# Attention with all score tiles turned by DMA, maxima taken in pairs, head pairs joined by a ratio of sums, and some MLP preparation on VectorE

## The chip, the core and the metric

The kernel runs on one core of a Trainium2 chip. The core has five engines, each working through its own list of instructions in order: TensorE (PE, with its weight loads shown apart as PEld), VectorE (DVE), ScalarE (ACT), GpSimd (POOL) and SyncE (SP), which here issues the DMAs. Engines wait for each other by semaphores. PE writes to PSUM, of which there are eight banks of 512 fp32 columns for each of 128 partitions; the other data lie in SBUF, and 16 DMA engines move data between DRAM and SBUF and within SBUF. The metric is the device time in microseconds.

## What is computed

An adaptive-layernorm block over 2048 rows of width 576, of attention and a gated MLP, in fp32. Cut to what matters here:

```python
h = _layernorm(x) * (1 + ca) + sa
q = h @ wq                                  # 32 heads of 128
k, v = the last 512 rows of 16 cached heads, each used by two query heads
p = softmax(q k^T / sqrt(128))              # 512 columns a row
x = x + ga * (concat(p v) @ wo)
h = _layernorm(x) * (1 + cb) + sb
x = x + gb * ((silu(h @ w1) * (h @ w3)) @ w2)   # inner width 4608
```

## The kernel before

**Precision.** PE multiplies fp16. A value in fp32 is split into a high fp16 half and a low one (the value less the high half), and each product is made of three matmuls: high by high, high by low and low by high.

**Slots.** The rows lie in four blocks of 512, the block in four tiles of 128 rows. The attention is a list `slots` of 128 entries, (use of a key head, query head `j` of its two, block). One slot is one query head on one block; slots 2p and 2p + 1 are the two heads of a pair on the same block, so the second head (`j` = 1) is always in an odd slot. The loop near the end of the kernel goes over slots `i` and steps `t` of 0 to 3 and writes the instructions of every engine in that order. No scheduler moves them: the order is that of the code.

**One slot's work.** `query` projects a slot ahead (14 matmuls in three parts, `QP`). `scores(i, t)` makes one tile of scores in a PSUM bank (tag S, two of them), and DVE takes the maximum of each row and a bias from it. `weights` makes the exponents on ACT, with their sums in `l`. The exponents have to be turned for the product with the values. For tiles 0 to 2, `half_high` (ACT) and `half_low` (POOL) split them to fp16 and `turn_away` (SP) turns them by a DMA transpose into `ptw`. Tile 3 goes another way: `turn` has PE turn it in fp32 by four transposes into a bank of tag T, a slot later, and `turn_high` (ACT) and `turn_low` (DVE) split it. `values(i - 1)` stands at the end of slot i, with 12 matmuls, and needs all four tiles.

**Sums.** `sums` takes the reciprocals, writes them to DRAM and reads them back to all partitions (`r`, 256 KB). `normalize`, two slots later, multiplies the product by them into `on`, `split_on` splits `on` in two halves `o` (ACT copy, POOL subtraction), and `attend_out` multiplies both heads of a pair by `wo` in one PSUM pair of banks `E`, from which DVE adds to `acc`.

**Preparation beside it.** Tasks put at steps (`at`, `run`) run after the step's own work: loads and splits of the next heads' weights, and the preparation of the MLP's weights. `make_set` makes sums and differences of blocks of w1 and w3 (Strassen-like products), `make_rows` multiplies rows of w2 by a gate and does the same. An item of that plan is a cast on ACT (`wmade`, `omade`) and subtractions on POOL. The table `WORK` spreads the items: full rate in slots 16 to 80, half in 80 to 104, 0.6 of it in 104 to 123. In the attention POOL does the sums and gates; for the last `FEW` = 8 blocks, which are made in the MLP, DVE does.

**Buffers.** `p` (PB) and `hp` (HF) have four buffers each, `ptw` two. A buffer is written again once its last reader has finished.

Of the kernel before, what the change touches and what calls it, by code (L numbers as in the profile page):

```python
# [9 lines left out]
F32 = mybir.dt.float32  # L10
# [12 lines left out]
DC = 4  # L23
# [20 lines left out]
Q_DOWN = 2.0**-17  # L44
EXPONENT = 0x7F800000
# [3 lines left out]
def tile_block(  # L49
# [27 lines left out]
    def bank(tag, name):  # L77
        return psum.tile([P, 512], F32, tag=tag, name=name)
# [4 lines left out]
    tpool = turning.enter_context(tc.tile_pool(name="tpool", bufs=2, space=PSUM))  # L83

    def t_bank():
        return tpool.tile([P, 512], F32, tag="T", name="pt")
# [149 lines left out]
    def turn_rows(b, m, tag):  # L236

        ps = t_bank() if tag == "T" else bank(tag, "ps_n")
# [202 lines left out]
    QP = (range(0, 5), range(5, 10), range(10, 14))  # L441
# [33 lines left out]
    def scores(i, t):  # L475
# [4 lines left out]
        rows = slice(t * P, (t + 1) * P)  # L480
        pss = bank("S", "pss")
        for n, (x, y) in enumerate(((0, 0), (0, 1), (1, 0))):
            nc.tensor.matmul(pss, q[:, x, rows], k[:, y, :], start=n == 0, stop=n == 2)  # L483
        m = (i * ST + t) % 3
        nm = nms[:, 2 * m : 2 * m + 2]
        factor = factors[:, g, j : j + 1]
        nc.vector.tensor_reduce(nm[:, 0:1], pss, axis=AX.X, op=ALU.max, negate=True)  # L487
        nc.vector.tensor_scalar(nm[:, 1:2], nm[:, 0:1], factor, P_LOG, op0=ALU.mult, op1=ALU.add)  # L488
        st["max", t] = pss, nm

    def weights(i, t):
# [5 lines left out]
        if t == 0:  # L497
            st["l"] = odd.tile([P, 2 * ST], F32, tag="l", name="l", bufs=3)
        p = pool.tile([P, SB], F32, tag="p", name="p", bufs=PB)
        nc.scalar.activation(p, pss, AF.Exp, bias=nm[:, 1:2], scale=factor, accum_out=st["l"][:, t : t + 1])  # L500
        st["p", t] = p

    def sums(i, step):

        st = state[i]
        if step == 0:
            nc.vector.reciprocal(st["l"][:, ST:], st["l"][:, :ST])
        elif step == 1:
            st["row"] = dram.tile([P, ST], F32, name=f"row{i}")
            nc.sync.dma_start(st["row"], st["l"][:, ST:])  # L510
# [5 lines left out]

    def turn(i, t):

        st = state[i]
        p = st.pop(("p", t))  # L520
        ps = st["t"] = t_bank().rearrange("p (j n) -> p j n", j=KC)
        for j in range(KC):
            nc.tensor.transpose(ps[:, j, :], p[:, j * P : (j + 1) * P], ident)  # L523

    def turn_high(i, t):
        st = state[i]
        nc.scalar.copy(st["pt"][:, 0, :, t * P : (t + 1) * P], st["t"])
# [6 lines left out]
    def half_low(i, t):  # L534

        hp = state[i]["hp", t]
        nc.gpsimd.tensor_sub(hp[:, 1, :], state[i].pop(("p", t)), hp[:, 0, :])  # L537
# [10 lines left out]

    def turn_low(i, t):
        cols = slice(t * P, (t + 1) * P)  # L550
        pt = state[i]["pt"]
        nc.vector.tensor_sub(pt[:, 1, :, cols], state[i]["t"], pt[:, 0, :, cols])  # L552
# [13 lines left out]

    def normalize(i):
# [9 lines left out]
    def split_on(i):  # L577
        st = state[i]
        on = st.pop("on")
        o = st["o"] = pool.tile([P, 2, SB], F16, tag=("ah", "al")[i % 2], name="o", bufs=3)  # L580
# [3 lines left out]
    def attend_out(pair, t, j, total):  # L584
        u, _, b = slots[2 * pair]
        back(state[2 * pair + j]["o"], wos[u][:, j], t, j == 0, j == 1)
        if j == 1:
# [3 lines left out]
                a, E[:, :, :HALF], factors[:, uses[u][0], 2:3], a, op0=ALU.mult, op1=ALU.add  # L591
# [164 lines left out]
    def make_set(f, n):  # L756
# [3 lines left out]
        if n < 0:  # L760
            eng = nc.vector if f >= NF - FEW else nc.gpsimd
            eng.tensor_add(s1, a21, a22)
            eng.tensor_sub(s2, s1, a11)
# [41 lines left out]
    def make_rows(p, n):  # L805
# [3 lines left out]
        if n < 0:  # L809
            if n < -2:  # L810
                r = whole[:, 2 * n + 8 : 2 * n + 10, :]
                eng = nc.vector if 2 * p >= NF - FEW else nc.gpsimd
                eng.tensor_mul(r, r, half_split(gates["b"]))
# [865 lines left out]
```

## Time and profile before

| | us |
|---|---|
| three runs, median | 2773.86 |
| lowest and highest | 2771.83 and 2776.18 |
| the profiled execution | 2773.59 |
| its span, first to last instruction | 2771.7 |
| first and last start of the values' matmuls (L562) | 61.7 and 1612.9 |

The profile is of one execution. A row of a group gives the line, the engine, the operation, output and input by name with partitions and elements, the count, busy time and the mean duration in ns, then the idle time just before and what ended it. A row of the timeline gives start, length, engine, line and names. In a row with three durations these are the least, the median and the largest. A row of the waits gives who waited for whom, then the total, the number of times and the longest. Matmuls are pipelined, with their ends modelled: the length of a matmul goes on past the start of the next.

### The profile page before, as it was taken

Reading aid. Unit: us, or ns where it says so; the run is one execution under the profiler, and the core shown is the slowest. Engines: PE = TensorE matmul, PEld = TensorE weight load, DVE = VectorE, ACT = ScalarE, POOL = GpSimd, SP = SyncE. Lnnn points to the kernel's source line nnn. Section 1 sums busy time; section 2 is a strip of 40 time slices with the busy share of each in tenths; the row PEclk is TensorE's granted clock in tenths of the full one; section 3 lists DMA queues with packets and bytes.
Section 4 is the critical chain, followed back from the end, with each engine's and each line's share of the span. In section 5 each row is a group of like instructions: output and inputs, shape, how many; then the busy total and the mean of one; then the engine's idle time right before and its main releaser. Section 6 shows DMA issues by size and latency. Waiting matters only on the chain.

```text
span 2771.7 us, 44752 instructions
## 1 busy us (share of the span) xinstructions
PE 2692.8 (97%) x15406; PEld 1515.9 (55%) x15406; DVE 1999.8 (72%) x3555; ACT 1617.5 (58%) x3013; POOL 1881.9 (68%) x1748
## 2 busy tenths in 40 slices
PE   6899999999999999999999999999999999999998
PEld 3455555555555555555555555555555555555554
DVE  7877787877788787877876667777776666666666
ACT  5777778777777778787677634544443333333332
POOL 5578788888788877777669537688873465333435
PEclk8999999999999999999999999999999999999999
DMA  5778888788787788979889935656643434333332
GB/s 184 174 174 195 196 177 192 169 184 192 160 185 167 191 186 201 206 182 213 184 190 223 239 112 171 200 170 199 213 135 108 160 121 128 104 103 111 104 110 78
DMA packets 593460, 463.84 MB, mean 167 GB/s; under 512 B 442704, under 2 KB 472528, under 8 KB 592208
## 3 DMA queue, kind: packets, MB, share of 16 engines
q1 hardware_dynamic: 592944, 460.69, 64.9%
q8 instruction: 121, 1.98, 0.3%
q14 instruction: 107, 0.88, 0.1%
q10 hardware_dynamic: 288, 0.30, 0.0%
HBM read 264.19 MB, written 95.99 MB: 130 GB/s over the span
## 4 chain that ended last, share of the span: by engine, by line
PE 52%; DVE 2%; issue 1%; ACT 1%; POOL 1%; DMA 0%; SPq 0%; DVEq 0%; ACTq 0%; POOLq 0%
PE py L847 15%; PE px L847 11%; PE pe L932 7%; PE pf L932 7%; PE pe L433 3%; PE po L562 3%; PE pss L483 3%; PE pq L410 2%; PE pt L523 0%; PE pq L414 0%; DVE table L487 0%; DVE acc L590 0%; DVE on L571 0%; DMA r<-row 0%; ACT p L500 0%
## 5 line engine op out<-in xcount | busy, mean ns | idle before, releaser
L537 POOL TENSOR_TENSOR hp<-p,hp 128x512 f16<-128x512 f32 x384 | 450.2, 1175 | 271.0 <-ACT hp L532 147.9
L500 ACT ACTIVATE p<-pss,table,factors 128x512 f32<-128x512 f32 x512 | 396.9, 775 | 360.9 <-DVE table L488 186.6
L847 PEld LDWEIGHTS <-wset 128*128 128x128 f16 x3528 | 344.6, 98 | 337.9 <-issue 5.3
L487 DVE TENSOR_REDUCE table<-pss 128x1 f32<-128x512 f32 x512 | 350.3, 684 | 209.9 <-PE pss L483 205.9
L847 PE MATMUL py<-hset,wset 128*128 128x512 f16 x2016 | 483.6, 380 | 0.0
L433 PE MATMUL pe<-o 128*128 128x288 f16 x3072 | 459.6, 286 | 15.8 <-DVE acc L590 15.3
L483 PE MATMUL pss<-k,qT 128*128 128x512 f16 x1536 | 420.1, 381 | 13.7 <-ACT p L500 10.3
L433 PEld LDWEIGHTS <-o 128*128 128x128 f16 x3072 | 300.7, 98 | 189.6 <-issue 22.4
L562 PE MATMUL po<-ptw,v 128*128 128x512 f16 x1536 | 359.3, 382 | 10.4 <-DVE ptw L552 5.5
L847 PE MATMUL px<-hset,wset 128*128 128x512 f16 x1512 | 361.6, 379 | 1.6 <-ACT p L500 1.6
L410 PE MATMUL pq<-hT,wq 128*128 128x512 f16 x1092 | 283.2, 382 | 1.0 <-POOL hT L254 0.7
L94 POOL TENSOR_TENSOR akv<-u,akv 128x512 f16<-128x512 f32 x141 | 165.0, 1180 | 174.3 <-ACT akv L93 166.5
L532 ACT CAST hp<-p 128x512 f16<-128x512 f32 x384 | 237.3, 618 | 13.2 <-POOL hT L256 0.6
L562 PEld LDWEIGHTS <-v 128*128 128x128 f16 x1536 | 148.2, 98 | 175.4 <-issue 19.4
L932 PEld LDWEIGHTS <-akv 128*128 128x128 f16 x1728 | 169.6, 98 | 93.8 <-issue 4.8
L483 PEld LDWEIGHTS <-qT 128*128 128x128 f16 x1536 | 147.9, 98 | 129.0 <-issue 15.6
L590 DVE SCALAR_TENSOR_TENSOR acc<-pe,factors,acc 128x576 f32<-128x576 f32 x256 | 207.7, 811 | 10.4 <-PE pe L433 10.4
L582 POOL TENSOR_TENSOR o<-on,o 128x512 f16<-128x512 f32 x128 | 150.4, 1175 | 55.6 <-ACT o L581 52.7
L410 PEld LDWEIGHTS <-wq 128*128 128x128 f16 x1092 | 107.5, 98 | 129.7 <-issue 4.6
L926 DVE SCALAR_TENSOR_TENSOR acc<-pf,table,acc 128x576 f32<-128x576 f32 x140 | 113.4, 810 | 80.3 <-PE pf L932 80.3
L1027 ACT COPY u<-py 128x512 f32<-128x512 f32 x72 | 42.2, 586 | 202.1 <-PE py L847 200.2
L1020 ACT ACTIVATE s<-s,table 128x512 f32<-128x512 f32 x72 | 52.0, 722 | 173.9 <-DVE s L1019 173.9
(244 smaller groups left out, 4791.2 us busy)
## 6 DMA issues: line engine op xcount, KB each, us to landing
wset<-wd SPq DMA_DIRECT2D x213, 320.0 KB, 3.2
r<-row SPq DMA_DIRECT2D x128, 256.0 KB, 3.9
oset<-od SPq DMA_DIRECT2D x106, 288.0 KB, 3.2
wraw<-in_w SPq DMA_DIRECT2D x36, 768.0 KB, 5.7
wd<-wmade SPq DMA_DIRECT2D x75, 320.0 KB, 3.3
wset<-wd SPq DMA_DIRECT2D x71, 160.0 KB, 2.3
w2raw<-in_w SPq DMA_DIRECT2D x19, 576.0 KB, 5.3
wd<-ring SPq DMA_DIRECT2D x33, 320.0 KB, 2.8
```

Of the source, the lines that this page charges most:

```text
L94: eng.tensor_sub(halves[:, 1], src, halves[:, 0])
L410: nc.tensor.matmul(ps, w[:, k // 2, m, :], hT[:, DC + m if k == 1 else m, :], start=s == 0, stop=False)
L433: nc.tensor.matmul(E[:, h, :HALF], o[:, x, rows], w[:, y, h * HALF : (h + 1) * HALF], start=first and n == 0, stop=last and n == 2,)
L483: nc.tensor.matmul(pss, q[:, x, rows], k[:, y, :], start=n == 0, stop=n == 2)
L487: nc.vector.tensor_reduce(nm[:, 0:1], pss, axis=AX.X, op=ALU.max, negate=True)
L500: nc.scalar.activation(p, pss, AF.Exp, bias=nm[:, 1:2], scale=factor, accum_out=st["l"][:, t : t + 1])
L532: nc.scalar.copy(hp[:, 0, :], state[i]["p", t])
L537: nc.gpsimd.tensor_sub(hp[:, 1, :], state[i].pop(("p", t)), hp[:, 0, :])
L562: nc.tensor.matmul(po, v[:, x, c, :], pt[:, y, c, :], start=c == 0 and n == 0, stop=c == KC - 1 and n == 2)
L590: nc.vector.scalar_tensor_tensor(a, E[:, :, :HALF], factors[:, uses[u][0], 2:3], a, op0=ALU.mult, op1=ALU.add)
L847: nc.tensor.matmul(ps, w[:, a, :], h[:, b, :], start=start and n == 0, stop=stop and n == 6, skip_group_check=True)
L932: nc.tensor.matmul(ps[:, h, :HALF], a[:, rows], w[:, b, :], start=m == 0, stop=m == 2)
```

## The change

`scores` is called for even steps only and makes two tiles side by side in a pair of banks (tag T, two pairs). One reduction takes the maxima of both tiles, and one instruction both biases. `weights` and `half_high` run for both tiles of the pair in the odd step that follows. All four tiles are split by `half_high` and `half_low` and turned by DMA; `turn`, `turn_high` and `turn_low` are gone. The low half of tile 0 is made by DVE from the fourth slot on, those of tiles 1 to 3 by POOL, of which tiles 2 and 3 at the start of the next slot, and `turn_away` for them comes in steps 0 and 1 of the next slot.

A pair of heads keeps one `l`. The first head is no longer multiplied by its reciprocal sums: `take_first` (ACT) and `normalize` (DVE) split its product as it is, scaled by 2^-24. The second head is multiplied by the ratio of the first head's sum to its own, so only odd slots write a row to DRAM and read it to all partitions. `attend_out` multiplies by the first head's reciprocal when it adds to `acc`.

In the attention DVE now does `make_set`'s two first sums and the gates of `make_rows`; the other preparation stays. The parts of the query projection have 4, 6 and 4 matmuls in place of 5, 5 and 4, and the first steps of the kernel use the T banks in place of S. No group of instructions of the MLP changes; there, `px` uses two banks of tag S that are taken once the T pairs are given back.

On PE, at the start of step 1 of slot 63 before, where `pt` is a tile being turned, `pss` scores and `pq` a query projection:

```order
L433 MATMUL pe_76<-o_8805,o_9084 128x288
L523 MATMUL pt_9432<-ident_71,p_9372 128x128 x4
L483 LDWEIGHTS qT_9351
L483 MATMUL pss_9437<-k_8218,qT_9351 128x512
L483 LDWEIGHTS qT_9351
L483 MATMUL pss_9437<-k_8218,qT_9351 128x512
L483 LDWEIGHTS qT_9351
L483 MATMUL pss_9437<-k_8218,qT_9351 128x512
L410 LDWEIGHTS wq_9287
```

The same slot after, at its start, behind the values of slot 61:

```order
L562 MATMUL po_8636<-ptw_8448,v_7690 128x512
L493 LDWEIGHTS qT_8602
L493 MATMUL pss_8652<-k_7565,qT_8602 128x512
L493 LDWEIGHTS qT_8602
L493 MATMUL pss_8652<-k_7565,qT_8602 128x512
L493 LDWEIGHTS qT_8602
L493 MATMUL pss_8652<-k_7565,qT_8602 128x512
L493 LDWEIGHTS qT_8602
L493 MATMUL pss_8652<-k_7565,qT_8602 128x512
L493 LDWEIGHTS qT_8602
L493 MATMUL pss_8652<-k_7565,qT_8602 128x512
L493 LDWEIGHTS qT_8602
```

The transposes are gone from step 1, and the scores of two tiles stand together in step 0.

On ACT, slot 63 after, from the first exponents (`p`) of its second pair of tiles; `hp` is a high half, `on` the output of slot 61 and `omade` a block of prepared w2:

```order
L511 ACTIVATE p_8735,l_8555<-pss_8708,table_223,factors_101 128x512
L536 CAST hp_8737<-p_8735 128x512
L511 ACTIVATE p_8739,l_8555<-pss_8708,table_223,factors_101 128x512
L536 CAST hp_8741<-p_8739 128x512
L599 CAST o_8744<-on_8678 128x512
L817 CAST omade_8757<-w2raw_8211 128x2x288
L573 ACTIVATE o_8786<-po_8761 128x512
```

Before, the copy of the output stood behind the exponents of one tile of the slot; now it, and the cast of `omade` behind it, stand behind two.

On POOL, slots 62 and 63 before, where `hp` is a low half and `o` the subtraction of the output:

```order
L537 TENSOR_TENSOR hp_9411<-p_9409,hp_9411 128x512
L343 TENSOR_TENSOR wq_9427<-wraw_8922,wq_9427 128x640
L537 TENSOR_TENSOR hp_9447<-p_9445,hp_9447 128x512
L801 TENSOR_TENSOR omade_9465<-w2raw_8928,omade_9465 128x288
L537 TENSOR_TENSOR hp_9479<-p_9477,hp_9479 128x512
L582 TENSOR_TENSOR o_9510<-on_9443,o_9510 128x512
L801 TENSOR_TENSOR omade_9523<-w2raw_8928,omade_9523 128x2x288
L537 TENSOR_TENSOR hp_9550<-p_9548,hp_9550 128x512
```

And slot 63 after, whose low halves of tiles 1, 2 and 3 are `hp_8686`, `hp_8737` and `hp_8741`:

```order
L542 TENSOR_TENSOR hp_8686<-p_8684,hp_8686 128x512
L600 TENSOR_TENSOR o_8744<-on_8678,o_8744 128x512
L818 TENSOR_TENSOR omade_8757<-w2raw_8211,omade_8757 128x2x288
L542 TENSOR_TENSOR hp_8737<-p_8735,hp_8737 128x512
L542 TENSOR_TENSOR hp_8741<-p_8739,hp_8741 128x512
L542 TENSOR_TENSOR hp_8811<-p_8809,hp_8811 128x512
```

The low halves of tiles 2 and 3 now stand behind the output's subtraction and behind the item of the slot's last step.

The diff, cut to its core:

```diff
+O_DOWN = 2.0**-24
...
+    def pair_bank(name="pt"):
+        return tpool.tile([P, 2, 512], F32, tag="T", name=name)
...
-    QP = (range(0, 5), range(5, 10), range(10, 14))
+    QP = (range(0, 4), range(4, 10), range(10, 14))
...
-        pss = bank("S", "pss")
-        for n, (x, y) in enumerate(((0, 0), (0, 1), (1, 0))):
-            nc.tensor.matmul(pss, q[:, x, rows], k[:, y, :], start=n == 0, stop=n == 2)
...
+        pss = pair_bank("pss")
+        for half in range(2):
+            rows = slice((t + half) * P, (t + half + 1) * P)
+            for n, (x, y) in enumerate(((0, 0), (0, 1), (1, 0))):
+                nc.tensor.matmul(pss[:, half, :], q[:, x, rows], k[:, y, :], start=n == 0, stop=n == 2)
...
-        nc.vector.tensor_reduce(nm[:, 0:1], pss, axis=AX.X, op=ALU.max, negate=True)
-        nc.vector.tensor_scalar(nm[:, 1:2], nm[:, 0:1], factor, P_LOG, op0=ALU.mult, op1=ALU.add)
+        nc.vector.tensor_reduce(nm[:, 0:2], pss, axis=AX.X, op=ALU.max, negate=True)
+        nc.vector.tensor_scalar(nm[:, 2:4], nm[:, 0:2], factor, P_LOG, op0=ALU.mult, op1=ALU.add)
...
+        if j == 0:
+            return
+        first, both, up, ratio = (st["l"][:, lo * ST : hi * ST] for lo, hi in ((0, 1), (0, 2), (2, 4), (4, 5)))
         if step == 0:
-            nc.vector.reciprocal(st["l"][:, ST:], st["l"][:, :ST])
+            nc.vector.reciprocal(up, both)
+            nc.vector.scalar_tensor_tensor(ratio, first, O_DOWN, up[:, ST:], op0=ALU.mult, op1=ALU.mult)
...
-        nc.gpsimd.tensor_sub(hp[:, 1, :], state[i].pop(("p", t)), hp[:, 0, :])
+        eng = nc.vector if t == 0 and i > 2 else nc.gpsimd
+        eng.tensor_sub(hp[:, 1, :], state[i].pop(("p", t)), hp[:, 0, :])
...
+    def take_first(i):
+        st = state[i]
+        o = st["o"] = new_o(i)
+        nc.scalar.activation(o[:, 0, :], st["po"], AF.Copy, scale=O_DOWN)
...
+        if slots[i][1] == 0:
+            o = st["o"]
+            nc.vector.scalar_tensor_tensor(o[:, 1, :], po, O_DOWN, o[:, 0, :], op0=ALU.mult, op1=ALU.subtract)
+            return
...
-                a, E[:, :, :HALF], factors[:, uses[u][0], 2:3], a, op0=ALU.mult, op1=ALU.add
+                a, E[:, :, :HALF], state[2 * pair]["l"][:, 5 * ST + t : 5 * ST + t + 1], a, op0=ALU.mult, op1=ALU.add
...
-            eng = nc.vector if f >= NF - FEW else nc.gpsimd
-            eng.tensor_add(s1, a21, a22)
-            eng.tensor_sub(s2, s1, a11)
+            nc.vector.tensor_add(s1, a21, a22)
+            nc.vector.tensor_sub(s2, s1, a11)
...
-                eng = nc.vector if 2 * p >= NF - FEW else nc.gpsimd
-                eng.tensor_mul(r, r, half_split(gates["b"]))
+                nc.vector.tensor_mul(r, r, half_split(gates["b"]))
...
+            if t == 0 and 1 <= i <= n:
+                half_low(i - 1, 2)
+                half_low(i - 1, 3)
+            if t == 2 and i < n:
+                half_low(i, 0)
+                half_low(i, 1)
             if t > 1 and i < n:
                 turn_away(i, t - 2)
-            if t == 0 and 1 <= i <= n:
-                turn_away(i - 1, 2)
-            slot, tile = (i - 1 if t == 1 else n, ST - 1)
-            if 0 <= slot < n:
-                turn(slot, tile)
-            if i < n:
+            if t < 2 and 1 <= i <= n:
+                turn_away(i - 1, t + 2)
+            if t % 2 == 0 and i < n:
                 scores(i, t)
...
-            if i < n:
-                weights(i, t)
-            if t < 3 and i < n:
-                half_high(i, t)
-                half_low(i, t)
...
+            if t % 2 and i < n:
+                for k in (t - 1, t):
+                    weights(i, k)
+                    half_high(i, k)
+            if 2 <= i <= n + 1 and t == 0 and slots[i - 2][1] == 0:
+                take_first(i - 2)
```

More of the change, by code (lines that the diff above doesn't have):

```diff
@@ L515, in sums @@
             )
[L517 to L527, printed above, removed]
     def half_high(i, t):
@@ L1515, in tile_block @@
         norm_rows(0, t)
-    turned = [turn_rows(0, m, "TTAAS"[m]) for m in range(DC + 1)]
+    firsts = [pair_bank(), pair_bank()]
+    junk = firsts[1][:, 1, :]
+    turned = [
+        turn_rows(0, m, "A", None if m in (2, 3) else firsts[m // 4][:, m % 2, :]) for m in range(DC + 1)
+    ]
     for m in range(DC + 1):
@@ L1607, in tile_block @@
     lane[1] = (E, after.tile([P, 2, 512], F32, tag="T2", name="pf"))
+    later.append(after)
     for _ in stream:
```

50 lines of the change are left out of this document (27 added, 23 removed).

## The prediction

> **What bounds the kernel now.** I read the summary of the page first, then busy time by stage, then the order of time on TensorE in one steady stretch.
>
> ```profile
> span 2771.7 us, 44752 instructions
> PE 2692.8 (97%) x15406; PEld 1515.9 (55%) x15406; DVE 1999.8 (72%) x3555; ACT 1617.5 (58%) x3013; POOL 1881.9 (68%) x1748
> 300.00:1000.00 700.00, 684.88 (x3909) 381.32 (x3908) 552.69 (x1115) 543.53 (x1051) 596.25 (x572) 1.00 0.79 178
> 1000.00:1300.00 300.00, 295.93 (x1693) 164.65 (x1692) 237.46 (x477) 229.89 (x450) 229.20 (x208) 1.00 0.87 202
> 1500.00:1600.00 100.00, 92.73 (x522) 51.34 (x521) 59.84 (x115) 64.95 (x126) 64.79 (x58) 1.00 0.98 239
> 2300.00:2600.00 300.00, 300.00 (x1734) 169.43 (x1733) 183.44 (x239) 95.60 (x164) 126.60 (x105) 1.00 0.36 109
> ```
>
> The windows give busy us of PE, PEld, DVE, ACT and POOL, then granted clock, DMA share and GB/s. TensorE is the bound everywhere, at full clock. The attention (to about 1613 us) differs from the MLP (2300:2600): there POOL is 85% busy, DVE 79%, ACT 78% and DMA 79 to 98%, so a TensorE saving has little room above the other four. All of the change lies in the attention.
>
> ```profile
> 802.12 2.80 PE L562 MATMUL po<-ptw,v 128*128 128x512 f16 x12
> 806.49 0.90 PE L433 MATMUL pe<-o 128*128 128x288 f16 x6
> 807.22 0.60 PE L523 MATMUL pt<-ident,p 128*128 128x128 f32 x4
> 807.66 0.81 PE L483 MATMUL pss<-k,qT 128*128 128x512 f16 x3
> 808.31 1.24 PE L410 MATMUL pq<-hT,wq 128*128 128x512 f16 x5
> 809.38 0.90 PE L433 MATMUL pe<-o 128*128 128x288 f16 x6
> 810.12 0.81 PE L483 MATMUL pss<-k,qT 128*128 128x512 f16 x3
> 813.75 2.75 PE L562 MATMUL po<-ptw,v 128*128 128x512 f16 x12
> ```
>
> Starts, not durations, count here, since matmuls overlap. One slot (a head on one block) lasts 813.75 - 802.12 = 11.63 us. In it three score matmuls hold PE for 808.31 - 807.66 = 0.65 us (0.215 each of 512 columns), six of the output projection for 0.74, and the four transposes for 807.66 - 807.22 = 0.44.
>
> **What the change removes from PE.** The four transposes of 128 slots: 128 x 0.44 = **56.3 us**. The grouped row says 77.3 us; that counts overlapped ends, so I take the starts.
>
> ```profile
> L523 PE MATMUL pt<-ident,p 128*128 128x128 f32 x512 | 77.3, 274 | 0.0
> PE pss L483 <- ACT p L500: 10.3, 15, 2.5
> PE po L562 <- DVE ptw L552: 5.5, 8, 2.9
> PE po L562 <- DMA ptw<-hp: 3.2, 2, 2.4
> ```
>
> Two waits go too. Scores waited 10.3 us for the weights two tiles back to free a bank; a pair bank now waits for weights half a slot old. The values waited 5.5 us for the fourth tile's low half on DVE, which no longer exists. Together **15.8 us**. What is late next is the third wait, for the turned tiles.
>
> **The chain that must now fit.** All four tiles go exponent (ACT), high half (ACT), low half (POOL, the first on DVE), transpose (SP), and the values of a slot stand at the end of the next slot.
>
> ```profile
> L500 ACT ACTIVATE p<-pss,table,factors 128x512 f32<-128x512 f32 x512 | 396.9, 775 | 360.9 <-DVE table L488 186.6 <-issue 67.5 <-POOL o L582 30.7
> L500 ACT ACTIVATION_READ_ACCUMULATOR p<-pss,table,factors 128x1 f32 x512 | 98.7, 193 | 0.0
> L532 ACT CAST hp<-p 128x512 f16<-128x512 f32 x384 | 237.3, 618 | 13.2 <-POOL hT L256 0.6
> L537 POOL TENSOR_TENSOR hp<-p,hp x384: 1144/1159/1784, 40.3 to 1589.6; 128x512 f16<-128x512 f32 x192
> L487 DVE TENSOR_REDUCE table<-pss 128x1 f32<-128x512 f32 x512 | 350.3, 684 | 209.9 <-PE pss L483 205.9 <-PE pe L310 3.2
> L488 DVE TENSOR_SCALAR table<-table,factors 128x1 f32<-128x1 f32 x512 | 109.6, 214 | 18.2
> L305 DVE TENSOR_REDUCE top<-oraw 128x1 bf16<-128x1152 f32 x16 | 21.5, 1345 | 0.0
> L590 DVE SCALAR_TENSOR_TENSOR acc<-pe,factors,acc 128x576 f32<-128x576 f32 x256 | 207.7, 811 | 10.4 <-PE pe L433 10.4
> L581 ACT CAST o<-on 128x512 f16<-128x512 f32 x128 | 78.1, 610 | 7.1 <-DVE on L571 7.1
> L582 POOL TENSOR_TENSOR o<-on,o 128x512 f16<-128x512 f32 x128 | 150.4, 1175 | 55.6 <-ACT o L581 52.7 <-DMA h<-hf 0.9 <-POOL wmade L770 0.7
> DMA to landing us min/median/max: 3.0/3.9/8.2
> ```
>
> A reduction of 1024 columns is not in the trace. Between 512 (0.684) and 1152 (1.345) it is 1.21 by proportion, and at most two old ones, 1.37; I take 1.21. It saves 2 x 0.684 - 1.21 = 0.16 us of DVE a pair, and 0.21 for the second bias.
>
> Clock zero is the first score matmul of a slot, PE unhindered. Score pair to 1.29, four query matmuls 2.15, projection 2.89, six query 4.18, projection 4.92, second pair **6.21**, query 7.07, two projections 8.55, values 8.55 to **11.13**. DVE adds the projection of step 1 (4.92 + 0.81 = 5.73), takes the first low half (0.69 to 1.21, below; I take 1.21, as POOL is 85% busy), then reduction and bias: 6.94 + 1.42 = 8.36. ACT makes two exponents and two high halves, 2 x (0.97 + 0.62): 11.54. In an even slot the last low half ends at 12.7 and has landed 3.9 us after its issue, at 16.6; it is wanted at 11.13 + 8.55 = **19.68**. In an odd slot (second head) the output's copy stands behind the halves on ACT (12.15) and its subtraction ahead of the last two low halves on POOL: 12.15 + 1.175 + 2 x 1.16 = 15.65, landed at **19.55**. So even slots have 3.1 us to spare, odd ones 0.1, and each us of preparation that gets into an odd slot's chain is a us of waiting, once per two slots.
>
> The order listings above show one such slot: the cast of `omade` is behind the output's copy on ACT, its subtraction ahead of both low halves on POOL. With 1.28 us for that subtraction the tiles land 1.2 us late. The MLP plan has nearly two items a slot over four steps in slots 16 to 80, half as many in 80 to 104, so about half, then a quarter, of odd slots have one at this place.
>
> ```profile
> 817.90 1.28 POOL L801 TENSOR_TENSOR omade<-w2raw,omade 128x576 f16<-128x576 f32 x1
> ```
>
> I take 0.5 us a pair for that and 0.15 for a busy queue: 64 pairs x 0.65 = **42 us** given back. Bounds: 0, if the halves run earlier than drawn, and 1.4 (below).
>
> **Work moved between POOL and DVE.**
>
> ```profile
> L762 POOL TENSOR_TENSOR wraw<-wraw x28: 994/1002/1524, 205.5 to 1441.2; 128x384 f32<-128x384 f32 x28
> L762 DVE TENSOR_TENSOR wraw<-wraw x8: 539/548/1211, 1652.1 to 1972.3; 128x384 f32<-128x384 f32 x8
> L813 POOL TENSOR_TENSOR w2raw<-w2raw,gate_b x28: 1401/1410/1857, 256.1 to 1471.8; 128x576 f32<-128x576 f32 x28
> L813 DVE TENSOR_TENSOR w2raw<-w2raw,gate_b x10: 739/742/1399, 1713.8 to 2036.1; 128x576 f32<-128x576 f32 x10
> L94 DVE TENSOR_TENSOR aal<-u,aal x19: 692/1210/1280, 1662.8 to 2751.8; 128x512 f16<-128x512 f32 x19
> L552 DVE TENSOR_TENSOR ptw<-pt,ptw 128x512 f16<-128x512 f32 x128 | 87.5, 684 | 27.3 <-ACT ptw L527 25.7 <-DMA od<-omade 1.2
> ```
>
> POOL loses 56 sums at 1.0 and 28 gates at 1.41 (95 us) and half of the output subtractions (64 x 1.175 = 75): from 596/58 = 10.2 us a slot in 300:1000 (698 value matmuls, 12 a slot: 58 slots, by the rows under DMA) to about 8.7. DVE gets 56 x 0.55 + 28 x 0.74 = 51 us, at most 56 x 1.21 + 28 x 1.40 = 107, about 0.5 to 1.1 a slot, and 0.69 to 1.21 for the first low half. It loses the fourth tile's low half (0.68) and 2 x 0.37 of maxima and biases. Its 552.69/58 = 9.5 a slot becomes 9.3 to 10.4: below 11.13, hence no bound, and no cost beyond the places taken above. ACT keeps its count (a high half for a turned copy).
>
> DVE has two speeds here, 0.69 and 1.21 for one shape. [...]
>
> **DMA.** The rows are the value matmuls of two stages (busy and count on PE, then DVE) and the broadcasts' size.
>
> ```profile
> 300.00:1000.00 700.00, 162.90 (x698) 63.08 (x58) 1.00 0.79 178
> 1000.00:1300.00 300.00, 69.08 (x300) 28.33 (x26) 1.00 0.87 202
> r<-row SPq DMA_DIRECT2D x128, 256.0 KB, 3.9
> ```
>
> In 2300:2600, 0.36 x 300 us moved 109 x 300 us = 32.7 MB: 3.3 us of all engines per MB, 0.86 for 256 KB. In 300:1000 the bytes alone would give 178 x 0.0033 = 0.59; the other 0.20 x 700 us over 3 x 58 transposes is 0.81 each. A transpose then costs 1.67, a slot's change is +1.67 - 0.86/2 (half the broadcasts) = +1.24: 9.5 to 10.8 us a slot in 300:1000 (below 11.13), 0.87 x 12 + 1.24 = 11.7 in 1000:1300 (25 slots of 12.0 us now), and beyond the span in 1500:1600. There 8 slots add 10 us to a full queue; I take **8 us**, between 0 and 10.
>
> [...]
>
> **Sum**, against the profiled execution's 2773.6 us (0.3 below the median of three): 2773.6 - 56.3 - 15.8 + 42 + 8 = **2751 us**, 0.8% faster. The stretch before the first slot and the MLP, where no group changes, cost nothing either way.
>
> **Rivals.**
> - *All covered*: no wait for tiles, no DMA term: 2773.6 - 72.1 = 2702, with a few us of each left about 2712. For it: even slots have 3.1 us. Against it: the 0.1 us of odd ones. 13%.
> - *The odd slots' chain binds harder, slower*: the added transpose waits in a queue that is 93% full or more; half a transpose (0.8) in front raises 0.65 to 1.45 a pair, 93 us: 2773.6 - 72.1 + 93 + 8 = 2802. It decides from 1.0 us a pair (64 us, all that is won after DMA). [...] 26%.
> - *DMA sets the pace from 1000 us*: the 41 slots in 1000:1500 stay at their length, so that their share of the gain, 22.7/128 x 41 = 7 us, goes, and as much again where its queue delays loads earlier: 2765, reaching to no change (2770). For it: 0.87 to 0.98 now. 19%.
>
> **How the numbers follow.** Forecast 42%, the others as given. The range runs from the covered case to the slower one, 2712 to 2798; its tails beyond hold some 2 in 10. A measurement tells apart about 0.2%, 5.5 us: faster takes the forecast, the covered case and half of the DMA case, 0.64; the other half, 0.10, is the same; 0.26 slower.
>
> **What would show it.** Right: slots of about 11.2 to 11.6 us by the starts of the values, no transposes on PE, and the largest PE wait in the attention from DMA `ptw<-hp` ahead of the values of odd slots, some 40 us. Wrong upwards: that wait near 100 us, or PE waiting for `qT` or `acc` on DVE; DMA share at 0.95 or above from 300 us on. Wrong downwards: no such wait. The MLP from the first `py` on should last as before.

## The result, and the profile after

| | before | after |
|---|---|---|
| median, us | 2772.85 | 2926.72 |
| lowest and highest | 2771.61 and 2776.18 | 2926.13 and 2931.73 |
| ratio, 95% interval | | 1.0557 [1.0539, 1.0575] |

The changed kernel is 5.6% slower, 154 us, above the predicted range. The summary of the page of the changed kernel, and two windows of the attention with the columns of those before (PE, PEld, DVE, ACT, POOL, clock, DMA share, GB/s):

```profile
span 2925.5 us, 42892 instructions
PE 2685.7 (92%) x14894; PEld 1465.5 (50%) x14894; DVE 2122.6 (73%) x3188; ACT 1633.6 (56%) x3013; POOL 1756.5 (60%) x1603
300.00:1000.00 700.00, 619.79 (x3339) 326.33 (x3337) 568.62 (x872) 502.40 (x957) 476.06 (x442) 0.96 0.78 172
1000.00:1500.00 500.00, 445.97 (x2408) 235.92 (x2407) 387.44 (x618) 345.21 (x663) 308.87 (x277) 0.96 0.81 185
```

PE fell from 685 to 620 us in 300:1000: it now waits. The DMA share did not rise, so the queues as a whole do not set the pace here, and the granted clock fell from 1.00 to 0.96. Who is waited for is in the view of PE's waits (total, times, longest):

```profile
PE po L562 <- DMA ptw<-hp: 118.0, 55, 7.8
PE po L562 <- issue: 29.5, 13, 8.1
PE pe L442 <- DVE acc L608: 15.6, 16, 1.7
PE po L562 <- DMA row<-l: 12.2, 2, 8.5
PE pss L493 <- DVE qT L482: 7.7, 7, 2.0
PE pss L493 <- ACT p L511: 7.0, 9, 2.0
```

It was 3.2 us in all for the turned tiles before. "Issue" and `row` ahead of the same matmuls are the same wait under another name: in all 15 of these cases the last turned tile landed 0.09 to 0.25 us before the matmul started. Where the tiles are in time, a slot is as short as forecast; the values' rows of one such slot in the timeline:

```profile
729.68 2.75 PE L562 MATMUL po<-ptw,v 128*128 128x512 f16 x12 [1.18 <-issue]
740.82 1.46 PE L562 MATMUL po<-ptw,v 128*128 128x512 f16 x6
```

740.82 - 729.68 = 11.14 us. But only 12 of the 106 slots 17 to 122 take under 11.25, and their mean is 13.24. A slot that waits, an odd one, from the timelines of all engines:

```profile
855.50 0.59 PE L419 MATMUL pq<-hT,wq 128*128 128x512 f16 x2
855.87 1.38 DVE L829 TENSOR_TENSOR w2raw<-w2raw,gate_b 128x576 f32<-128x576 f32 x1
857.17 1.64 DVE L542 TENSOR_TENSOR hp<-p,hp 128x512 f16<-128x512 f32 x1
858.74 1.21 DVE L497 TENSOR_REDUCE table<-pss 128x2 f32<-128x1024 f32 x1
859.98 0.61 DVE L498 TENSOR_SCALAR table<-table,factors 128x2 f32<-128x2 f32 x1
860.27 4.44 PE L562 MATMUL po<-ptw,v 128*128 128x512 f16 x12 [2.27 <-DMA ptw<-hp]
863.53 0.61 ACT L599 CAST o<-on 128x512 f16<-128x512 f32 x1
864.23 1.16 POOL L600 TENSOR_TENSOR o<-on,o 128x512 f16<-128x512 f32 x1 [3.65 <-ACT o L599]
865.34 1.16 POOL L786 TENSOR_TENSOR wmade<-wraw,wmade 128x512 f16<-128x512 f32 x1
866.58 0.67 POOL L787 TENSOR_TENSOR wmade<-wraw,wmade 64x256 f16<-64x256 f32 x1
867.33 0.79 POOL L831 TENSOR_TENSOR w2raw<-w2raw 128x288 f32<-128x288 f32 x1
868.20 0.79 POOL L832 TENSOR_TENSOR w2raw<-w2raw 128x288 f32<-128x288 f32 x1
868.95 2.27 POOL L542 TENSOR_TENSOR hp<-p,hp 128x512 f16<-128x512 f32 x2
871.41 0.57 SPq L737 DMA_DIRECT2D wd<-wmade  x1
872.09 1.30 SPq L549 DMA_TRANSPOSE ptw<-hp  x1
875.54 2.75 PE L562 MATMUL po<-ptw,v 128*128 128x512 f16 x12 [2.28 <-DMA ptw<-hp]
```

The second score pair's last matmul starts just before the query's at 855.50. VectorE first does a moved gate (1.38 us) and the first low half (1.64 us, of 0.67 at best: it ended 0.55 us after POOL's instruction, which ran to 858.26, see the last section), so the reduction starts at 858.74. After the exponents POOL has, ahead of the two low halves, the output's subtraction and four pieces of preparation: they start at 868.95, 4.8 us after the output's copy on ACT ended (864.14). A store stands between the two turns on SP. The values wait 2.28 us. The values of the slot before, at 860.27, show the other loss: 12 matmuls in 4.44 us in place of 2.75, in part at half clock (mean granted clock 0.61 in 860.27:864.70).

For every matmul I took the time from its start to the next start, less the median of its line. The sum of these excess gaps is 101 us before and 310 after. Ahead of and inside the blocks of values they went from 18 to 220: 171 of waits, in 78 of 128 blocks (92 in odd slots, 79 in even ones), and about 46 in 27 blocks that ran in part at half clock. The rest moved by 7. So +209, less the 56 us of transposes, is the 153 us of loss.

### The profile page after: what moved, and what is told of

Read it like the earlier page. It is cut to its first block, busy times and chain, and to the rows that moved or that the text cites. A ratio compares the mean times of both kernels' runs of the same rounds, so it can differ in the third digit from the quotient of the medians.

```text
span 2925.5 us, 42892 instructions
## 1 busy us (share of the span) xinstructions
PE 2685.7 (92%) x14894; PEld 1465.5 (50%) x14894; DVE 2122.6 (73%) x3188; ACT 1633.6 (56%) x3013; POOL 1756.5 (60%) x1603
## 4 chain that ended last, share of the span: by engine, by line
PE 55%; DVE 13%; DMA 7%; issue 7%; POOL 6%; ACT 4%; SPq 1%; POOLq 0%; ACTq 0%; DVEq 0%
PE py L863 15%; PE px L863 10%; PE po L562 7%; PE pe L948 6%; PE pf L948 6%; DMA ptw<-hp 6%; PE pss L493 4%; PE pe L442 3%; DVE table L497 3%; PE pq L419 3%; POOL hp L542 3%; DVE table L498 2%; ACT p L511 2%; DVE hp L542 1%; DVE acc L608 1%
## 5 line engine op out<-in xcount | busy, mean ns | idle before, releaser
L562 PE MATMUL po<-ptw,v 128*128 128x512 f16 x1536 | 401.2, 417 | 161.8 <-DMA ptw<-hp 118.0
L542 POOL TENSOR_TENSOR hp<-p,hp 128x512 f16<-128x512 f32 x387 | 462.7, 1209 | 126.5 <-ACT hp L536 96.7
L497 DVE TENSOR_REDUCE table<-pss 128x2 f32<-128x1024 f32 x256 | 311.5, 1217 | 251.6 <-PE pss L493 251.3
L442 PE MATMUL pe<-o 128*128 128x288 f16 x3072 | 439.7, 286 | 18.0 <-DVE acc L608 15.6
L493 PE MATMUL pss<-k,qT 128*128 128x512 f16 x1536 | 379.5, 383 | 15.5 <-DVE qT L482 7.7
L442 PEld LDWEIGHTS <-o 128*128 128x128 f16 x3072 | 300.3, 98 | 167.5 <-issue 23.5
L863 PE MATMUL px<-hset,wset 128*128 128x512 f16 x1470 | 351.5, 379 | 0.0
L536 ACT CAST hp<-p 128x512 f16<-128x512 f32 x512 | 316.4, 618 | 51.1 <-DMA ptw<-hp 32.9
L608 DVE SCALAR_TENSOR_TENSOR acc<-pe,l,acc 128x576 f32<-128x576 f32 x256 | 207.2, 810 | 52.5 <-PE pe L442 36.5
L600 POOL TENSOR_TENSOR o<-on,o 128x512 f16<-128x512 f32 x64 | 74.1, 1158 | 186.0 <-ACT o L599 173.9
L498 DVE TENSOR_SCALAR table<-table,factors 128x2 f32<-128x2 f32 x256 | 150.6, 588 | 9.1
```

The costliest lines, as they stand in the source:

```text
L442: nc.tensor.matmul(E[:, h, :HALF], o[:, x, rows], w[:, y, h * HALF : (h + 1) * HALF], start=first and n == 0, stop=last and n == 2,)
L493: nc.tensor.matmul(pss[:, half, :], q[:, x, rows], k[:, y, :], start=n == 0, stop=n == 2)
L497: nc.vector.tensor_reduce(nm[:, 0:2], pss, axis=AX.X, op=ALU.max, negate=True)
L498: nc.vector.tensor_scalar(nm[:, 2:4], nm[:, 0:2], factor, P_LOG, op0=ALU.mult, op1=ALU.add)
L536: nc.scalar.copy(hp[:, 0, :], state[i]["p", t])
L542: eng.tensor_sub(hp[:, 1, :], state[i].pop(("p", t)), hp[:, 0, :])
```

## The experiments

The kernel before ran beside each at 2771 to 2774 us. My theory after the result: the chain from the second score pair to the turned tiles is longer than its room (the work that PE has between those scores and the values), above all since low halves stand behind preparation on POOL. The rivals: VectorE's new work, the DMA queues, or the half clock as a cause in itself.

### Parts of the change in the kernel before

**e4_fourth**: only the fourth tile turned by DMA; its transposes on PE and its halves from PSUM on ACT and DVE go.

```diff
-            slot, tile = (i - 1 if t == 1 else n, ST - 1)
-            if 0 <= slot < n:
-                turn(slot, tile)
+            if t == 1 and 1 <= i <= n:
+                turn_away(i - 1, ST - 1)
...
-            if t < 3 and i < n:
+            if i < n:
                 half_high(i, t)
```

> The kernel before with one part of the change alone: the fourth tile too is split by ACT and POOL and turned by DMA (its transpose in step 1 of the next slot); PE's transposes, ACT's and DVE's halves of the turned tile go. Scores stay single, the sums and the preparation stay where they were. PE loses 56 us. Theory D: the fourth transpose alone makes the values late, 2850 or more. Theory Q: the fourth low half adds 1.16 us of POOL a slot to a POOL at 85%, so the tiles are late as well, 2800 to 2900, with POOL above 90% busy. If the pairs are to blame (both tiles of a pair start together, 1.2 us later): 2720 to 2760.

2831.54 us, 1.0213 [1.0184, 1.0243].

**e8_mlp_dve**: only the sums and gates on VectorE.

```diff
-            eng = nc.vector if f >= NF - FEW else nc.gpsimd
+            eng = nc.vector
```

> The kernel before with one part of the change alone: DVE makes the two sums of each pair of w1 and w3 blocks and the gates of w2 in the attention. Theory Q (POOL's queue): 95 us less on POOL, little to win since the chain of before has about 7 us of room: 2765 to 2775. [...]

2832.97 us, 1.0221 [1.0205, 1.0236].

**e11_fourth_mlp**: both edits.

> The kernel before with two parts of the change: the fourth tile by DMA (e4, +59 us) and the sums and gates on DVE (e8, +61 us). If POOL's queue is what e4 suffers from, the relief is worth some 30 us or more, and the two together cost less than their sum: 2800 to 2860. If they add: 2880 to 2900.

2854.00 us, 1.0299 [1.0272, 1.0325]. Alone, either part costs about 60 us; together 83. A window and a wait of e4, then four waits of e8:

```profile
300.00:1000.00 700.00, 642.83 (x3529) 341.17 (x3527) 503.03 (x1008) 529.82 (x1012) 634.73 (x608) 0.99 0.89 193
PE pe L433 <- DVE acc L590: 37.8, 27, 3.4
```

```profile
PE pe L433 <- DVE acc L590: 21.4, 17, 3.8
PE po L562 <- DVE ptw L552: 17.5, 15, 3.0
PE pss L483 <- DVE qT L473: 15.0, 10, 2.9
DVE wraw L762 <- ACT wraw L1156: 67.8, 28, 4.0
```

In e4 POOL is at 635 of 700 us and the DMA share at 0.89: two candidates. That e11 costs 37 us less than both parts added is what I had expected of a POOL queue, but waits that overlap would give it too. In e8 VectorE, in order, stands 67.8 us before ACT's input to the sums, and PE waits longer for work of VectorE: 17.5 us for the turned tile's low half (5.5 before) and 15.0 for the query's (1.6 before). That the first makes the second was not tested.

**e18_fourth_vector** was meant to tell the two of e4 apart: the fourth low half on VectorE, as the turned tile's was, but in step 0 of the slot. The turned tile's stood in step 2, not where the expectation puts it.

```diff
-        nc.gpsimd.tensor_sub(hp[:, 1, :], state[i].pop(("p", t)), hp[:, 0, :])
+        eng = nc.vector if t == ST - 1 else nc.gpsimd
+        eng.tensor_sub(hp[:, 1, :], state[i].pop(("p", t)), hp[:, 0, :])
...
+            if t == 0 and 1 <= i <= n:
+                half_low(i - 1, ST - 1)
```

> e4_fourth (the kernel before with only the fourth tile turned by DMA) with the low half of that tile on VectorE at the start of the next slot, where VectorE made the turned tile's low half before, in place of on POOL. POOL then has the work of the kernel before, VectorE too, and TensorE 56 us less. Theory (e4's loss of 59 us came of POOL, which went to 91% busy in 300:1000): the time falls from 2831 to 2730 to 2775, the waits of the projection for acc (37.8 us) and of the scores for p (21.9) to about those before. Rival (the extra transpose in the DMA queues, or the hp buffers that it holds, made the loss): the time stays above 2800, with DMA at 0.95 or more in 1000:1500 and the waits on ptw or p as in e4.

2823.55 us, 1.0184 [1.0171, 1.0198]: the signs of the rival came. Its windows, its largest PE waits and one of VectorE's:

```profile
300.00:1000.00 700.00, 655.22 (x3601) 347.62 (x3599) 554.02 (x1084) 539.35 (x1031) 601.80 (x561) 0.99 0.90 197
1000.00:1500.00 500.00, 473.84 (x2653) 256.17 (x2652) 394.41 (x792) 373.31 (x716) 370.97 (x335) 1.00 0.95 213
...
PE po L563 <- DMA ptw<-hp: 30.2, 18, 5.0
PE pss L483 <- ACT p L500: 28.6, 43, 2.6
...
DVE hp L538 <- ACT hp L532: 32.6, 35, 6.5
```

POOL is back at 602 of 700 us (596 before), yet only 8 us came back. The DMA share is at 0.90 and 0.95, and tiles come late. That the full queues make them late is likely but not shown: VectorE now also stands 32.6 us for the fourth tile's high half, ahead of its reductions, and neither was tried alone. Whether the scores' wait for the exponents comes of buffers that the transposes hold was not tried. In the changed kernel half of the broadcasts are gone and the share stays at 0.78 to 0.81, but there PE is also slower.

**e3_mlp_pool**: the changed kernel with the sums and gates back on POOL.

```diff
-            nc.vector.tensor_add(s1, a21, a22)
+            eng = nc.vector if f >= NF - FEW else nc.gpsimd
+            eng.tensor_add(s1, a21, a22)
```

> The changed kernel with the sums of w1 and w3 blocks and the gates of w2 back on POOL. Theory Q: POOL's queue grows by 95 us in the attention, most of it ahead of low halves, so the waits before the values grow: 2950 to 3000. [...] Theory D: no change within 10 us.

2938.97 us, 1.0601 [1.057, 1.0632]: 12 us slower than the changed kernel. There the move to VectorE is a gain and not the cause of the loss, though e8 shows that it is a loss in the kernel before.

### The chain made shorter

**e1_early**: the low halves of tiles 2 and 3 right behind their high halves, a step earlier, and so ahead of the next preparation on POOL.

```diff
-            if t == 0 and 1 <= i <= n:
-                half_low(i - 1, 2)
-                half_low(i - 1, 3)
...
                     half_high(i, k)
+                if t == 3:
+                    half_low(i, 2)
+                    half_low(i, 3)
```

> The changed kernel with one move: the low halves of tiles 2 and 3 stand on POOL right behind the step that makes their high halves, ahead of the output's subtraction and of the step's preparation, in place of the start of the next slot. Theory Q (the tiles land late since their low halves queue behind preparation on POOL; in the changed kernel 2.7 us pass between the last high half and the low half of tile 2 in odd slots, 1.9 in even ones): about 2 us a slot leave the chain, the 171 us of waits before the values fall below 60 and the time to about 2800. [...] Theory D (the fourth transpose, SP and DMA): the landings stay late, above 2890.

2828.64 us, 1.0203 [1.0167, 1.0239]: 98 of the 154 us.

```profile
PE po L562 <- DMA ptw<-hp: 49.0, 24, 5.2
PE pe L442 <- DVE acc L608: 19.9, 20, 2.1
```

The wait for the tiles falls from 118.0 to 49.0 with no other edit: POOL's order is the largest cause.

**e2_onecol**: the pair's bias by two instructions of one column.

```diff
-        nc.vector.tensor_scalar(nm[:, 2:4], nm[:, 0:2], factor, P_LOG, op0=ALU.mult, op1=ALU.add)
+        for half in range(2):
+            nc.vector.tensor_scalar(
+                nm[:, 2 + half : 3 + half], nm[:, half : half + 1], factor, P_LOG, op0=ALU.mult, op1=ALU.add
+            )
```

> The changed kernel with the biases of a pair made by two instructions of one column each in place of one of two columns (588 ns mean in the changed kernel; one column took 214 before). Theory P: the two-column form waits for POOL; two short ones take about 0.43 and never wait, the spread of 0.23 to 0.87 goes, and 0.2 us leave the chain of each pair: 2890 to 2915. Theory Q and D: no more than that, 2905 to 2930. [...]

2903.99 us, 1.0475 [1.0444, 1.0505]: 23 us faster. The durations (least, median, largest) in the changed kernel, then in e2:

```profile
L498 DVE TENSOR_SCALAR table<-table,factors x256: 227/540/1411, 38.5 to 1741.3; 128x2 f32<-128x2 f32 x128
```

```profile
L499 DVE TENSOR_SCALAR table<-table,factors x512: 201/209/216, 38.7 to 1715.4; 128x1 f32<-128x1 f32 x171
```

One instruction of two columns takes 0.54 us in the median and up to 1.41; two of one column start 0.13 us apart and are done in 0.33 to 0.34.

**e9_two**: e1 and e2 together.

> The changed kernel with the edits of e1 and e2 together. If each takes its part out of the same chain (theory C), the sum is less than that of both (98 and 23 us): 2800 to 2815. If one-column biases help DVE, which is 87% busy in e1 and holds up projections and queries, the waits for acc and qT (63 us of TensorE by start times in e1) fall too: 2780 to 2800.

2812.15 us, 1.0148 [1.0118, 1.0177]: 41 us over the kernel before, the best of these.

**e12_two_pool**: e9 with the sums and gates back on POOL.

> As e9, with sums and gates back on POOL. With the low halves ahead of the preparation, POOL's longer queue no longer holds up the tiles, while DVE (87% busy in e1) is relieved: 2750 to 2790 if DVE is what binds in e9, and above e9 if it is still POOL.

2826.15 us, 1.0198 [1.0175, 1.0221], 14 slower than e9, as in e3. PE's waits and one of SP's in e9:

```profile
PE po L565 <- DMA ptw<-hp: 47.4, 24, 4.4
...
SPq L552 <- DVE hp L545: 248.3, 96, 7.9
```

What is left is the same wait, plus half clock: 99 us of excess gaps around the values, where 18 stood before (about 76 of waits and 22 at half clock, against 171 and 46 in the changed kernel); scores and projection are at 25 and 24 (21 and 21 before).

**e13_sp_order**: e9 with the first low half on POOL, and the last two turns next to each other on SP.

```diff
-        eng = nc.vector if t == 0 and i > 2 else nc.gpsimd
+        eng = nc.gpsimd
...
-            if t < 2 and 1 <= i <= n:
-                turn_away(i - 1, t + 2)
+            if t == 0 and 1 <= i <= n:
+                turn_away(i - 1, 2)
+                turn_away(i - 1, 3)
```

> e9_two with the first tile's low half back on POOL and the turns of the third and fourth tile issued right behind each other on SP at the start of the next slot. Theory (SP standing for VectorE's first low half, and a store between the two turns, delay the last turn by about 1.5 us): the wait of the values for the turned tiles falls from 74 us to below 40, the time from 2812 to about 2780. Rival (the remaining delay is VectorE's and ScalarE's own): values' wait stays within 15 us of 74 and the time within 10 us of 2812; slower still if POOL's extra 0.9 us a slot delays the other low halves.

2857.55 us, 1.0308 [1.0288, 1.0327]: the theory missed, and the last case that I had named, slower through POOL's extra work, came.

```profile
PE po L565 <- DMA ptw<-hp: 70.8, 24, 8.2
...
SPq L552 <- POOL hp L545: 606.3, 247, 23.6
```

SP now stands for POOL. Two edits went in at once, so which of them costs is open, and so is whether SP's wait for VectorE made the rest in e9.

### The room made longer

**e5_late** puts the values behind the query of step 1 of the next slot, and what uses them two steps later.

```diff
-        if 1 <= i <= n:
-            values(i - 1)
...
                 query(i + 1, t)
+            if t == 1 and 2 <= i <= n:
+                values(i - 2)
```

> The changed kernel with the values of a slot moved behind the query of step 1 of the slot after next (some 6.8 us later on TensorE; the first head's copy, the normalization and what hangs on it follow one or two steps later). No operation is added or taken away. Theory C (the loss is the length of the chain from the second pair of scores to the turned tiles, about 17 us against 13.5 us of TensorE work): with 6.8 us more room, less than the time of this move can be seen in waits, the 171 us of waits before the values and the slow clock behind them go, and the time is 2710 to 2760. Theory T (throughput: an engine or the DMA queues cannot go faster than a slot of about 13 us): the wait shows up elsewhere, 2860 or more.

2983.10 us, 1.0761 [1.074, 1.0783], a miss:

```profile
PE pss L493 <- DVE qT L482: 212.3, 116, 5.1
```

The values at the slot's end had covered the query's low half on VectorE. They had two uses, and I had seen one.

**e6_all0** (e9 with the values behind the query of step 0) and **e7_all1** (e9 with e5's place).

> The changed kernel with three edits: early low halves of tiles 2 and 3 (as in e1), one-column biases (e2), and the values behind the query of step 0 of the slot after next (2.2 us of TensorE work later). Theory C: e1 left about 65 us of waits before the values; 2.2 us of room more and 0.4 us less of chain take most of them, 2730 to 2770. Theory T: no better than e1, 2810 or more.

> As e6, with the values behind the query of step 1 (as in e5): all three edits. Theory C: no waits before the values are left, and TensorE loses only the projections' and queries' waits on DVE: 2700 to 2740, faster than both kernels. Theory T: 2800 or more. If DVE becomes the bound (early low halves and 86% of DVE's time): waits for qT and acc of 60 us and more, 2760 to 2790.

2948.75 us, 1.0637 [1.0616, 1.0659], and 2937.12, 1.0592 [1.0574, 1.0609]. In e7 the excess around the values is 4 us and that ahead of the scores 243: a shorter chain does not mend the lost cover.

**e10_shift**: e9 with the second pair's scores in step 1, and its weights, halves and turns as early as that allows.

```diff
-            if t % 2 == 0 and i < n:
-                scores(i, t)
+            if t < 2 and i < n:
+                scores(i, 2 * t)
```

> As e9, with the chain of the second pair begun a step earlier: its scores stand in step 1 in place of 2, its exponents, halves and transposes a step earlier as well; values and queries stay at their places, so that nothing loses the cover that e5 took away. Theory C: 2 to 3 us of room more before the values takes what waits e9 has there (98 us of excess by start times in e1): 2700 to 2750. If DVE is the bound once the tiles are in time: 2770 to 2800, with the waits at acc and qT. Theory T: as e9.

2872.23 us, 1.0366 [1.0339, 1.0393], a miss. Two of its waits:

```profile
PE pe L442 <- DVE acc L611: 46.3, 59, 2.7
PE po L565 <- DMA ptw<-hp: 37.0, 21, 6.7
```

The tiles come somewhat sooner, and the projection now waits for VectorE's additions; what holds these up was not followed.

**e14_query_first** makes the query in two steps in place of three, which takes PE work out of the room.

```diff
+    QQ = (range(0, 7), range(7, 14))
...
-            if t == 3 and i + 1 < n:
+            if i + 1 < n and t == len(qsteps(i + 1)):
                 query_low(i + 1)
```

> e9_two with each query's products in two steps in place of three, so that the query and its low half on VectorE are done a step earlier; the values stay at the end of the slot. It moves PE work away from between the second pair's scores and the values. Theory (the chain's room is the PE work between the second pair's scores and the values): with 4 chunks of the query (1.7 us a chunk set, some 0.9 to 3.5 us) less in that room, the values' wait grows from 74 us to over 150 and the time to above 2850; the waits of the scores for the query (12 us in the changed kernel) go. Rival (waits are set by the total load): within 15 us of 2812.

2848.62 us, 1.0278 [1.0256, 1.0301]. Slower by 36 us, as the room's theory has it, and within 2 us of the time that I had named. But the values' waits grew from about 76 to 93 us of excess gaps only, not to over 150, and the scores' wait for the query did not go (8.9 us, 9.2 in e9). So the theory has the sign and not the size.

**e15_query_first_late** is e14 with the values behind step 0's query, **e16_all_covers** that with e13's edits, and **e17_query_low_first** e16 with the query's low half ahead of the second reduction on VectorE.

```diff
+            if i + 1 < n and t == len(qsteps(i + 1)):
+                query_low(i + 1)
             if t == 2 and i < n:
                 half_low(i, 0)
```

> e14_query_first with the values behind the first query step of the next slot, a step later than at the slot's end. If the loss of e5 and e6 was the query's lost cover alone, this keeps both covers: values' wait below 15 us, scores' wait for the query below 30 us, time 2740 to 2775, about the kernel before. Rival (the scores then wait for the query all the same, since VectorE's order puts its low half behind the second pair's reductions): wait of the scores for the query above 100 us and the time above 2850.

> e15_query_first_late with e13's first low half on POOL and SP's order. If e15 holds: within 10 us of e15, since the values then wait for nothing. If e13's theory holds and e15's values still wait: 10 to 30 us faster than e15.

> e16_all_covers with the query's low half on VectorE ahead of the reduction of the second score pair, in place of behind it. Theory (in e15 and e16 the next slot's scores wait because VectorE, in order, does the second pair's reduction and bias, 1.5 us, and the multiplication for the head pair or its low half, 0.7 to 1.1 us, before the query's low half): the wait of the scores for VectorE's qT falls from 167 us to below 40 us and the time from 2938 to 2760 to 2800. Rival (the low half then delays the second pair's reduction and its exponents, and the waits move to the scores' bank or to the values): the sum of the two waits stays above 100 us and the time above 2850.

3024.98 us, 1.092 [1.0899, 1.0941]; 2938.16, 1.0599 [1.0582, 1.0616]; 2877.97, 1.0383 [1.0352, 1.0413]. The scores' waits in e15, then in e17:

```profile
PE pss L497 <- DVE qT L486: 261.1, 119, 6.8
```

```profile
PE pss L497 <- ACT qT L480: 55.3, 53, 3.0
PE pss L497 <- DVE qT L486: 15.7, 11, 2.4
PE pe L442 <- DVE acc L615: 15.4, 18, 1.7
...
PE po L569 <- DMA ptw<-hp: 6.8, 4, 3.5
```

e15's theory failed and its rival came. e16 was 87 us faster than e15, outside both of its cases; it too had two edits at once. e17's theory half held: VectorE's order was the wait (167.5 us in e16, 15.7 here), but only 60 us came back, and ACT's high half of the query is late next. With the tiles in time (6.8), the query is late; with the query in time, the tiles are. No version here beats the kernel before.

## Why the prediction was wrong

**Transposes, 56.3 us: right.** Slots of 11.14 us occur, 0.49 below the 11.63 of before.

**Two waits, 15.8 us: half right.** The values' wait for VectorE is gone; the scores' wait for the weights only fell from 10.3 to 7.0, and that for VectorE's `qT` grew from 1.6 to 7.7.

**The chain, "64 pairs x 0.65 = 42 us given back": the step that failed.** Measured: 171 us of waits, 2.7 a pair, and in even slots, which I gave 3.1 us to spare, nearly as much as in odd ones. From the end of the second scores to the values, means over slots 18 to 121 from the records' starts and lengths, beside my own lengths:

| piece, us | mine, odd / even | measured, odd / even |
|---|---|---|
| scores end to reduction | 0.73 | 1.55 / 1.60 |
| reduction and bias | 1.42 | 1.91 / 1.87 |
| two exponents and high halves | 3.18 | 3.46 / 3.16 |
| last high half to first of two low halves | 1.79 / -1.16 | 2.67 / 1.85 |
| two low halves | 2.32 | 2.38 / 2.40 |
| last low half to its turn's issue | 0 | 0.86 / 1.28 |
| issue to values | 3.9 | 4.18 / 4.74 |
| sum | 13.3 / 10.4 | 17.0 / 16.9 |

The unhindered room is 19.68 - 6.21 = 13.5 us. No single piece broke it. I had taken 1.21 us for the first low half since POOL is busy, when no run had shown that POOL's work sets it; it took 0.67 to 1.70 us, 0.89 in the median, and 80 of the 83 that started while a POOL instruction ran ended 0.55 to 0.65 us after it did. I let the chain wait for preparation at one spot of odd slots only, and ran it otherwise as if POOL and SP were free at each hand-over. Each stood behind other work in its order: POOL first (e1, 98 us), then the bias (e2, 23 alone, 16 more on top of e1).

The term that I had mis-sized most is the preparation on POOL, 0.5 us a pair. In the order of POOL there stood, between the low halves of tiles 1 and 2, a mean of 1.9 us of preparation in odd slots, beside the output's subtraction, and 2.1 us in even slots, where I had put none. Once the high half of tile 2 was ready, its low half started 4.3 us later in odd slots and 3.3 in even ones. For 2.5 and 1.6 us of this POOL worked on other pieces; for the other 1.8 and 1.7 it stood idle ahead of such a piece, mostly until ACT had made its input. So even the idle time of POOL was time in a queue. For the 41 us left in e9 the place is shown, the values; the cause is not.

**"Below 11.13, hence no bound": wrong inference.** In 300:1000 the blocks of values below count 636/12 = 53 slots:

```profile
300.00:1000.00 700.00, 165.51 (x636) 64.05 (x636) 0.96 0.78 172
```

568.62/53 = 10.7 us of VectorE a slot, against my 9.3 to 10.4. That is below 11.14 us too, but 96% of it, and VectorE was seldom free when the chain reached it: in slots 18 to 121 it stood idle ahead of 4 of the 104 reductions of second score pairs (72 of 104 for the first pairs). e8 fits this: it only moved work from POOL to VectorE and lost 61 us.

**The half clock: a term that I had left out.** By the granted clock, (1 - 0.974)/0.5 x 2925.5 = 152 us ran at half clock, against (1 - 0.992)/0.5 x 2771.7 = 44. Half of the difference, 54 us, is lost work (the 7 blocks of values wholly at half clock took 4.64 to 4.67 us from first to last start, against 2.37); 46 of it is seen in the values. It shrank with the waits (clock 0.985 in e1 and e9); no run takes the two apart.

**DMA, 8 us: not seen as such in the changed kernel**, whose share fell. The price of a transpose held, though. The queue's rows of before, then of e18 (packets, MB, share):

```profile
q1 hardware_dynamic: 592944, 460.69, 64.9%
```

```profile
q1 hardware_dynamic: 728112, 494.26, 70.8%
```

(0.708 x 2821.7 - 0.649 x 2771.7)/128 = 1.55 us of all 16 engines for each added transpose, against my 1.67. At a share of 0.95 from 1000 us in e18, the queues are, by my estimate from that share alone, the likely next bound of a version of this change that gets its tiles in time; no run shows it.

**The rivals.** The one on the other side had the right mechanism, a chain that binds harder, but at 1.45 us a pair, in odd slots, by the queue. The sign "that wait near 100 us" came: 118.0. The MLP lasts as before, as forecast: from the start of the last values to that of the last matmul 1154.2 us before, 1154.5 after.

## What to carry to other kernels

Lay a chain across engines against its room with each engine's queue as it stands, not with the engine free. Here VectorE, ACT and POOL had work for 96, 85 and 81% of the shortest slot (busy time in 300:1000 over 53 slots of 11.14 us), and the four hand-overs of the chain took 0.3 to 3.0 us each more than I had laid out. When work goes off the bounding engine, its slot gets shorter (here 11.63 to 11.14 us) and so does the room of every chain that was covered by it. Before moving a block later to give one chain room, ask which other chain it covers; the values covered the query.

## What the runs showed of the hardware

- In the changed kernel's trace TensorE's granted clock is 1.0 or 0.5, and it fell to 0.5 at some short waits. Blocks of values took 3.4 to 4.7 us in place of 2.37 (first to last start) after waits of 2.1 to 8.7 us, once after 0.97; yet 16 blocks with waits of 1.5 to 4.0 us ran at full clock. Of the 33 stretches at half clock 20 were 3.4 us long and 11 twice that. What decides which wait is followed by such a stretch is not shown.
- A VectorE instruction on two float32 columns took 0.23 to 1.41 us, one on one column 0.20 to 0.22. In the changed kernel's trace the 55 of two columns that met no POOL instruction took 0.23 us each, and of the 196 that started while one ran, 166 ended 0.02 to 0.05 us after it did. By their ends these 166 waited for POOL's running instruction; why, no run shows.
- The first low half, 128x512 from SBUF to SBUF on VectorE, shows the same: 0.67 to 0.70 us when no POOL instruction ran at its start, and of the 83 that started while one ran, 80 ended 0.55 to 0.65 us after it did. So the "two speeds" of the prediction are, for this operation, one speed and a wait.
